# Retention and a rational feed-forward block on one core: a list scheduler in the kernel sets the order of all engines, and decoding's words move from PSUM to SBUF

## The chip, the core and the metric

The kernel runs on one core of a Trainium2 chip, whose engines run side by side, each through its own queue in order: TensorE (PE: matmuls, and PEld: weight loads), VectorE (DVE), ScalarE (ACT), GpSimd (POOL), and SyncE (SP), which here issues every DMA. The metric is device microseconds of one execution. Lower is better.

## What is computed

A retention (linear attention with a decay for each head) over batch 4, 8 heads, 768 positions and 64 dimensions, and then a feed-forward block with a rational activation on the 3072 tokens of 512 values:

```
for t in range(S):
    state = gamma * state + k[:, :, t] outer v[:, :, t]
    y[:, :, t] = scale * q[:, :, t] @ state            # x: (3072, 512)
h = x @ w_in                                           # 512 -> 2048
P = a[0] + a[1]*h + a[2]*h**2 + a[3]*h**3
Q = 1 + |b[0]|*|h| + |b[1]|*h**2
out = (P / (Q + 1e-6)) @ w_out                         # 2048 -> 512
```

The weights arrive as 8-byte words, and the kernel decodes them to float32 on the chip.

## The kernel before

**Work.** The tokens are 24 chunks of 128 (6 for each of 4 batches), 4 chunks make a block of 512 tokens, 6 blocks in all. The hidden 2048 are 16 tiles f of 128. A *slot* is one pair (block n, tile f), 96 of them. Blocks 0 and 1 go through tiles 0 to 7 and then 8 to 15 (half sums of the output go to DRAM and come back); blocks 2 to 5 go through all 16.

**A chunk of retention.** TensorE computes scores `pa` (`scores`), VectorE masks them into `aT` (`mask`), GpSimd scales v (`scale_v`) and the state (`scale_state`). TensorE adds into `px` what the state recalls (`recall`), the values (`values_early`, `values_late`) and, for the next state, k outer v (`outer`). VectorE scales `px` (L329), ScalarE rounds it to `xh` (L330), VectorE forms the remainder `xl` (L334). Chunks follow each other through the state.

**A slot.** `gemm_in` (L392) multiplies xh, xl with the two parts of w_in's tile into a bank `ph`: 12 matmuls. ScalarE takes |h| (L403), q's inner term s (L409, or on GpSimd L405 where a tile is decoded and no chunk is due) and p (L411). GpSimd forms q = q*s (L410), VectorE the polynomial (L415, L416), ScalarE the reciprocal from a root (L420, L421), VectorE refines and multiplies (L424 to L426). The last one frees the bank `ph`, of which there are two. ScalarE rounds the result to `gh` (L431), GpSimd forms the remainder `gl` (L432), and `gemm_out` (L447) multiplies both with w_out's tile into four banks `po`: 12 matmuls.

**Decoding a weight tile** (32 tiles of 512 KB): ScalarE makes `t` from the word's low byte (L130) and `u` from its high half (L138), VectorE joins them (L146, L149), ScalarE rounds to `w` (L159), GpSimd forms the remainder (L166). `u` lives in a PSUM bank, which `u_bank` picks: early in free banks, later in the two that `pa` and `px` use too.

**Order.** It is written out by hand: `opening` does chunks 0 to 3 with two filler matmuls in each chunk and 10 ahead (they compute nothing that is used), and `run` then goes through the slots, one tile decoded in each, with the second product three slots behind (`LAG = 3`). Loads go out in program order on SP.

Of the kernel before, what the change touches and what calls it, by code (L numbers as in the profile page):

```python
# [7 lines left out]
F32 = mybir.dt.float32  # L8
F32R = mybir.dt.float32r
# [8 lines left out]
TB = 512  # L18


@with_exitstack
def tile_retention_rational_ffn(
# [24 lines left out]
    NB = NSTEP // SPB  # L47

# [16 lines left out]

    def early_bank(name, tag, dtype=F32):
        pool = ps_o if tag.startswith("po") else ps
        return pool.tile([P, TB], dtype, name=name, tag=tag)

    def u_bank():  # L70

        if not opened:
            return early_bank("u", "ph0", U32)
        if len(opened) < 2:
            count["u"] += 1
            return early_bank("u", f"po{count['u'] % 2}", U32)
# [24 lines left out]
    lead, HF = 4, NF // 2  # L101
    tiles = []
    for h in range(0, NF, HF):
        tiles += [(0, h + f) for f in range(lead)]
        for f in range(h, h + HF):
            tiles += [(1, f)] + [(0, f + lead)] * (f + lead < h + HF)
    raws = []

    def fetch(count=1):
        for m, f in tiles[len(raws) : len(raws) + count]:  # L110
            raw = wp.tile([P, DM, 2], U32, name="raw", tag=f"w{m}_{f}")
            nc.sync.dma_start(
                out=raw.rearrange("p m w -> p (m w)"), in_=(w_in, w_out)[m][f]
            )
            raws.append(raw)

    us, ts = {}, {}

    def decode_read(i):
        decode_low(i)  # L120
        decode_high(i)

    def decode_low(i):
        if i >= len(tiles):
            return


        ts[i] = ff.tile([P, DM], U32, name="t", bufs=3)
        byte = raws[i].rearrange("p m w -> p (m w)").bitcast(U8)[:, 3::8]
        nc.scalar.activation(ts[i], byte, AF.Identity, bias=lcon[:, 0:1], scale=1.0 / 32)  # L130

    def decode_high(i):
        if i >= len(tiles):
            return


        us[i] = u_bank()
        nc.scalar.activation(  # L138
            us[i].bitcast(F32), raws[i][:, :, 1].bitcast(F32), AF.Abs, scale=2.0 ** -112
        )  # L140

    def decode_join(i):
        if i >= len(tiles):
            return
        u = us.pop(i)
        nc.vector.scalar_tensor_tensor(  # L146
            u, u, 3, ts[i], ALU.logical_shift_left, ALU.bitwise_or
        )
        nc.vector.scalar_tensor_tensor(  # L149
            ts[i], raws[i][:, :, 1], 0x80000000, u, ALU.bitwise_and, ALU.bitwise_or  # L150
        )

    def decode_split(i):
        if i >= len(tiles):
            return
        m, f = tiles[i]

        w = (w1, w2)[m][f] = wp.tile([P, 2, DM], F32R, name="w", tag=f"w{m}_{f}")
        nc.scalar.copy(w[:, 0], ts[i].bitcast(F32))  # L159

    def decode_rest(i):
        if i >= len(tiles):
            return
        m, f = tiles[i]
        w = (w1, w2)[m][f]
        nc.gpsimd.tensor_sub(w[:, 1], ts.pop(i).bitcast(F32), w[:, 0].bitcast(F32))  # L166


    steps = {}
    x_tiles = {}  # L170

    def x_block(n):
        if n not in x_tiles:
            x_tiles[n] = (
                xp.tile([P, NP, TB], F32R, name="xh"),
                xp.tile([P, NP, TB], F32R, name="xl"),
            )
        return x_tiles[n]

    borrowed = {2: ("gh", "gh", "q", "gl", "s"), 3: ("gh", "gl", "q", "gl", "s")}

    def landing(i, which, name, shape):
        if i in borrowed:
            tag = borrowed[i][which]
            full = ff.tile([P, TB], F32, name=name, tag=tag, bufs=BUFS.get(tag, 2))
            return full.rearrange("p (a b) -> p a b", b=shape[2])[:, : shape[1]]
        return at.tile(shape, F32, name=name)

    def load_part(i, n, src, which, shape):
# [8 lines left out]
    def load_again(i):  # L200
        if i % C > 0:
            load_part(i, "q2T", q2T, 4, [P, 2, P])

    def load_rest(i):
        load_part(i, "qT", qT, 1, [P, NP, P])
        load_again(i)
        load_part(i, "v", v, 3, [P, H, D])
        if i % C < C - 1:
            load_part(i, "k", kk, 2, [P, H, D])

    def scale_v(i):
        st = steps[i]
        nc.gpsimd.tensor_mul(  # L218
            st["v"], st["v"], vdec_sb.unsqueeze(2).broadcast_to([P, H, D])
        )  # L220

    def scale_state(i):
        if i % C > 0:
            nc.gpsimd.tensor_mul(
                state, state, sdec_sb.unsqueeze(2).broadcast_to([P, NP, D])
            )
# [10 lines left out]
    def scores(i):  # L237
        st = steps[i]
        pa = [bank("pa")[:, : 6 * D].rearrange("p (j t) -> p j t", t=3 * D) for _ in range(2)]
        for j in range(2):  # L240
            for a in range(2):
                whole, part = [], []
                for s in range(2):
                    r = s ^ a
                    kt, qt = (st[n][half(s), 2 * a + j] for n in ("kT", "qT"))
                    to = pa[s][half(r), j, : 3 * D if a != s else 2 * D]
                    if a != s:
                        to = to.rearrange("p (x t) -> p x t", t=D)[:, ::2]
                        qt = qt.rearrange("p (x t) -> p x t", t=D)
                    whole.append((to, kt[:, :D], qt))  # L250
                    qt = st["qT"][half(s), 2 * a + j]
                    part.append((pa[s][half(1 - r), j, later(a, s)], kt[:, D:], qt[:, D:]))
                for to, kt, qt in part + whole if a else whole + part:
                    nc.tensor.matmul(to, kt, qt, start=True, stop=True, skip_group_check=True)  # L254
        st["pa"] = pa

    def mask(i):
        st = steps[i]
        for s in range(2):
            st["aT", s] = at.tile([P, 2, 3 * D], F32, name="aT")  # L260
            nc.vector.tensor_mul(
                st["aT", s], st["pa"][s],
                causal_sb.rearrange("p x t -> p (x t)").unsqueeze(1).broadcast_to([P, 2, 3 * D]),
            )

    def outer(i, early=False):
        st = steps[i]
        px = st["px"]
        if i % C < C - 1:
            pk = st["pk"] = px[1][:, TB // 2 :].rearrange("p (h d) -> p h d", d=D)  # L270
            for aj in range(NP):
                for r in range(2):
                    h = 4 * (aj // 2) + 2 * r + aj % 2
                    nc.tensor.matmul(  # L274
                        pk[half(r), aj], st["k"][:, h], st["v"][:, h],
                        start=(i % C == 0 or early), stop=True, skip_group_check=True,
                    )

    def recall(i):
        st = steps[i]  # L280
        if i % C > 0:

            for a in range(2):
                for j in range(2):
                    for r in range(2):
                        qt = st["q2T"][half(r), j] if a else st["qT"][half(r), j]
                        nc.tensor.matmul(  # L287
                            st["px"][r][half(j), a * P : (a + 1) * P], state[half(r), 2 * a + j], qt,
                            start=(a == 0), stop=False, skip_group_check=True,
                        )  # L290
# [392 lines left out]
```

## Time and profile before

| | us |
|---|---|
| median of 3 runs | 639.15 (638.56 to 639.27) |
| profiled execution, its time | 639.73 |
| its span in the profile | 638.0 |
| TensorE busy | 611.7 (96%) |
| VectorE busy | 452.9 (71%) |
| ScalarE busy | 441.4 (69%) |
| GpSimd busy | 334.2 (52%) |

A row of the table by stretches has, for each engine, its busy time in that stretch and how many instructions; then the clock that TensorE was granted (1.00 is full), the share of time in which the DMA engines were busy, and GB/s. A row of a timeline has start, duration, engine, line, operation and operands, with the idle time ahead of it and what ended that in brackets. A row of the groups has line, engine, operation, operands, count, then busy us and mean ns of one, then the idle time ahead and what ended it.

### The profile page before, as it was taken

The numbers are of one execution on the slowest core, as the hardware profiler recorded it, in microseconds if no ns is written. First come the engines' busy times: TensorE is split into PE (matmuls) and PEld (weight loads), VectorE is DVE, ScalarE is ACT, GpSimd is POOL, SyncE is SP. The second block draws the span as 40 slices with busy tenths as digits, with TensorE's granted clock in tenths as the row PEclk, the third lists the DMA queues.
The fourth block names the chain that finished last, engine by engine and source line by source line (L and its number), as shares of the span: only waits on it lengthen the run. The fifth ranks groups of instructions, "written<-read, shape, count | busy, mean of one in ns | idle before, by whom it ended". The sixth has DMA issues, their size and how long they took to land.

```text
span 638.0 us, 11577 instructions
## 1 busy us (share of the span) xinstructions
PE 611.7 (96%) x4506; PEld 494.4 (77%) x4510; DVE 452.9 (71%) x731; ACT 441.4 (69%) x721; POOL 334.2 (52%) x288
## 2 busy tenths in 40 slices
PE   6766999999999999999999999999999999999997
PEld 4655778888877878788888888888878888888885
DVE  3778688888888666785666777667766766666664
ACT  2488789888886665567666675766766666777773
POOL 1566568887875543454453454535354443444442
PEclk9887999999999999999999999999999999999999
DMA  8995563101015232320120311111311000100001
GB/s 306 393 370 174 192 241 141 44 1 66 1 45 180 87 96 85 124 76 17 59 59 17 116 44 61 48 27 54 112 40 43 2 0 1 42 25 2 0 2 66
DMA packets 27270, 55.11 MB, mean 86 GB/s; under 512 B 3408, under 2 KB 6096, under 8 KB 27216
## 3 DMA queue, kind: packets, MB, share of 16 engines
q1 hardware_dynamic: 27216, 54.38, 25.1%
q8 instruction: 35, 0.57, 0.4%
q14 instruction: 19, 0.16, 0.1%
HBM read 45.98 MB, written 8.39 MB: 85 GB/s over the span
## 4 chain that ended last, share of the span: by engine, by line
PE 67%; ACT 13%; DVE 11%; issue 5%; DMA 2%; POOL 1%; SPq 1%; POOLq 0%; DVEq 0%; ACTq 0%
PE po L447 30%; PE ph L392 30%; ACT t L130 3%; ACT s L420 2%; ACT ph L421 2%; DVE q L424 2%; PE pa L254 2%; DVE p L426 2%; DVE ph L425 2%; PE px L308 2%; DMA v<-in_v 2%; PE px L287 2%; PE px L274 1%; ACT u L138 1%; ACT s L409 1%
## 5 line engine op out<-in xcount | busy, mean ns | idle before, releaser
L410 POOL TENSOR_TENSOR q<-q,s 128x512 f32<-128x512 f32 x96 | 124.4, 1296 | 224.1 <-ACT s L409 215.4
L392 PE MATMUL ph<-xh,w 128*128 128x512 f32 (+2 forms) x776 | 210.4, 393 | 10.1 <-DVE p L426 5.7
L447 PE MATMUL po<-w,gh 128*128 128x512 f32 x768 | 201.4, 394 | 0.0
L392 PEld LDWEIGHTS ph<-xh,w 128*128 128x128 f32 x776 | 143.8, 188 | 42.5 <-DVE t L149 3.0
L447 PEld LDWEIGHTS po<-w,gh 128*128 128x128 f32 x768 | 143.4, 189 | 30.7 <-POOL w L166 0.2
L403 ACT ACTIVATE q<-ph 128x512 f32<-128x512 f32 x96 | 57.2, 596 | 111.3 <-PE ph L392 111.2
L415 DVE TENSOR_TENSOR p<-ph,p 128x512 f32<-128x512 f32 x96 | 66.2, 689 | 94.1 <-ACT p L411 94.1
L432 POOL TENSOR_TENSOR gl<-p,gh 128x512 fp32r<-128x512 f32 x96 | 124.4, 1295 | 9.7 <-ACT gh L431 3.8
L447 PE MATMUL po<-w,gl 128*128 128x512 f32 x384 | 111.1, 391 | 0.2 <-POOL gl L432 0.2
L424 DVE SCALAR_TENSOR_TENSOR q<-q,small,ph 128x512 f32<-128x512 f32 x96 | 71.4, 744 | 47.3 <-ACT ph L421 47.2
L392 PE MATMUL ph<-xl,w 128*128 128x512 f32 (+2 forms) x388 | 104.1, 390 | 0.0
L420 ACT ACTIVATE s<-q,small 128x512 f32<-128x512 f32 x96 | 69.4, 723 | 22.7 <-POOL q L410 22.7
L392 PEld LDWEIGHTS ph<-xl,w 128*128 128x128 f32 x388 | 73.2, 189 | 15.4
L447 PEld LDWEIGHTS po<-w,gl 128*128 128x128 f32 x384 | 72.5, 189 | 15.8 <-POOL gl L432 0.6
L416 DVE SCALAR_TENSOR_TENSOR p<-p,small,ph 128x512 f32<-128x512 f32 x96 | 71.8, 748 | 3.4
L411 ACT ACTIVATE p<-ph,small 128x512 f32<-128x512 f32 x96 | 73.2, 762 | 0.0
L425 DVE SCALAR_TENSOR_TENSOR ph<-p,small,ph 128x512 f32<-128x512 f32 x96 | 72.0, 750 | 0.0
L431 ACT CAST gh<-p 128x512 fp32r<-128x512 f32 x96 | 58.6, 610 | 16.7 <-DVE p L426 16.7
L426 DVE SCALAR_TENSOR_TENSOR p<-q,ph 128x512 f32<-128x512 f32 x96 | 65.9, 687 | 3.3
L409 ACT ACTIVATE s<-q,small 128x512 f32<-128x512 f32 x80 | 65.3, 816 | 2.7
L421 ACT ACTIVATE ph<-s 128x512 f32<-128x512 f32 x96 | 57.8, 602 | 9.9 <-DVE p L416 0.8
L218 POOL TENSOR_TENSOR v<-v,small 128x512 f32<-128x512 f32 x24 | 25.0, 1044 | 41.8 <-DMA v<-in_v 40.1
(41 smaller groups left out, 439.8 us busy)
## 6 DMA issues: line engine op xcount, KB each, us to landing
raw<-in_w_in SPq DMA_DIRECT2D x16, 512.0 KB, 5.7
raw<-in_w_out SPq DMA_DIRECT2D x16, 512.0 KB, 7.3
kT<-in_kT SPq DMA_DIRECT2D x24, 256.0 KB, 2.8
qT<-in_qT SPq DMA_DIRECT2D x24, 256.0 KB, 3.2
v<-in_v SPq DMA_DIRECT2D x24, 256.0 KB, 3.6
out<-o SPq DMA_DIRECT2D x24, 256.0 KB, 2.1
k<-in_k SPq DMA_DIRECT2D x20, 256.0 KB, 3.9
q2T<-in_q2T SPq DMA_DIRECT2D x20, 128.0 KB, 3.2
```

What stands on the lines that cost most here:

```text
L392: nc.tensor.matmul(ph[:, t0:t1], w1[f][:, part, kt * P : (kt + 1) * P], x[:, kt, t0:t1], start=(i == 0), stop=(i == 3 * NP - 1),)
L409: nc.scalar.activation(s, q, AF.Identity, bias=babs[:, 0:1], scale=babs[:, 1:2])
L410: nc.gpsimd.tensor_mul(q, q, s)
L411: nc.scalar.activation(p, ph, AF.Identity, bias=par_sb[:, 2:3], scale=par_sb[:, 3:4])
L416: nc.vector.scalar_tensor_tensor(p, p, par_sb[:, 1:2], ph, ALU.add, ALU.mult)
L420: nc.scalar.activation(s, q, AF.Abs_reciprocal_sqrt, bias=qcon[:, 0:1])
L421: nc.scalar.activation(ph, s, AF.Square)
L424: nc.vector.scalar_tensor_tensor(q, q, qcon[:, 0:1], ph, ALU.add, ALU.mult)
L425: nc.vector.scalar_tensor_tensor(ph, p, par_sb[:, 0:1], ph, ALU.add, ALU.mult)
L426: nc.vector.scalar_tensor_tensor(p, q, 2.0, ph, ALU.subtract, ALU.mult, reverse0=True)
L432: nc.gpsimd.tensor_sub(gl, p, gh.bitcast(F32))
L447: nc.tensor.matmul(o_tiles[n][tt], g_[:, tt * P : (tt + 1) * P], w2[f][:, part], start=(first and m == 0), stop=(last and m == 2),)
```

## The change

All steps become objects: each has the engines that may run it, a cost, the steps that it follows, a rank, the buffers that it takes and those that it uses. `Plan.order` then repeats: for each engine it finds the step that could begin first by its own clock of costs, takes among those within `LOOK` of it the one of lowest rank, and issues the earliest over all engines. The order so found is the program's order. The arithmetic and the number of its instructions stay, but for filler matmuls and where the step s runs. What is different beside the order:

- `u` of the decoding is an SBUF tile of the pool that also holds outputs (`o`, 4 buffers), and no PSUM bank.
- The banks: ph has b0 and b1, pa and px have pairs of the others (b2 and b3 once two first products are under way), po has b4 to b7.
- The step s may go to GpSimd or ScalarE in slots below `SHARED = 30`, whichever can begin first (19 go to GpSimd, 16 before).
- The second product's rank is its slot plus 3.6 (`OUT`); it runs when it is ready and no step of lower rank is.
- In the opening the k outer v of chunks 1 to 3 is a step of its own, and scores may run up to two chunks ahead.
- Fillers go wherever the plan sees a gap on TensorE of 0.6 us or more before the first product.

```diff
+class Plan:
+    def ready(self, x):
+        t = 0
+        for a, early in x.after:
+            if a.start is None:
+                return None
+            t = max(t, a.start if early is None else a.end - early + WAKE)
...
+    def order(self, before=None):
+        waiting = list(self.steps)
+        while waiting:
...
+                for e in x.engines:
+                    start = max(t, self.free.get(e, 0))
+                    if e == "SP" and len(self.landings) >= LANES:
+                        start = max(start, self.landings[-LANES])
+                    by_engine.setdefault(e, []).append((start, x.rank, len(by_engine), x))
+            for e, found in by_engine.items():
+                first = min(f[0] for f in found)
+                start, rank, _, x = min(
+                    (f for f in found if f[0] <= first + LOOK.get(e, 0)), key=lambda f: (f[1], f[0])
+                )
+                if best is None or start < best[0]:
+                    best = start, e, x
...
-        us[i] = u_bank()
-        nc.scalar.activation(
-            us[i].bitcast(F32), raws[i][:, :, 1].bitcast(F32), AF.Abs, scale=2.0 ** -112
-        )
+            cell["u"] = ff.tile([P, DM], U32, name="u", tag="o", bufs=BUFS["o"])
+            nc.scalar.activation(
+                cell["u"].bitcast(F32), cell["raw"][:, :, 1].bitcast(F32), AF.Abs, scale=2.0 ** -112
+            )
...
+        L = step(("ACT",), (651, 761), low, [got], rank, [t])
+        U = step(("ACT",), (548, 623), high, [got, L], rank - 0.001, [u])
+        J = step(("DVE",), (1300, 1385), join, [L, U], rank, uses=[t, u])
+        S = step(("ACT",), (509, 607), split, [J], rank - 0.002, uses=[t])
+        R = step(("POOL",), (1249, 1295), rest, [S], rank, uses=[t])
...
+        A1 = turn("A1", step(("ACT",), (490, 600), a1, [G], k, [q], [ph]))
+        engines = ("ACT", "POOL") if k < SHARED else ("ACT",)
+        A2 = turn("A2", step(engines, {"ACT": (720, 820), "POOL": (771, 771)}, a2, [A1, ready["babs"]], k, [s], [q]))
+        A3 = turn("A3", step(("ACT",), (660, 760), a3, [G, A1, ready["par"]], k, [p], [ph]))
+        P1 = step(("POOL",), (1250, 1297), p1, [A2], k, uses=[q, s])
+        D1 = step(("DVE",), (1440, 1440), d1, [A3], k, uses=[p, ph])
+        A4 = step(("ACT",), (1265, 1327), a4, [P1, D1], k, uses=[q, s, ph])
+        D2 = step(("DVE",), (2030, 2100), d2, [A4, D1], k, uses=[p, q, ph])
+        A6 = turn("A6", step(("ACT",), (526, 610), a6, [D2], k, [gh], [p]))
+        P2 = turn("P2", step(("POOL",), (1253, 1297), p2, [A6], k, [gl], [p, gh]))
...
+        slack = 450 if first or final else 1800
+        O = step(
+            ("PE",), 2720, run_out,
+            [A6, (P2, slack), s1, (r1, slack), G, *gemms_out[-1:]], k + OUT,
+            [po] if first else [], [gh, gl] + ([] if first else [po]),
+        )
...
+LOOK = {"ACT": 100, "DVE": 100, "POOL": 100}
+EARLY = 2
+SHARED = 30
+OUT = 3.6
+AHEAD = 1.0
```

On SP's queue, the loads from chunk 1 to the first load of chunk 3 (kT, qT, q2T, v, k are a chunk's; raw is a weight tile). Before:

```order
L195 DMA kT<-in_kT 128x512
L195 DMA qT<-in_qT 128x512
L195 DMA q2T<-in_q2T 128x256
L195 DMA v<-in_v 128x512
L195 DMA k<-in_k 128x512
L112 DMA raw<-in_w_in 128x1024
L195 DMA kT<-in_kT 128x512
L195 DMA qT<-in_qT 128x512
L195 DMA q2T<-in_q2T 128x256
L195 DMA v<-in_v 128x512
L195 DMA k<-in_k 128x512
L112 DMA raw<-in_w_in 128x1024
```

Now:

```order
L221 DMA q2T<-in_q2T 128x256
L221 DMA raw<-in_w_in 128x1024
L221 DMA kT<-in_kT 128x512
L221 DMA qT<-in_qT 128x512
L221 DMA v<-in_v 128x512
L221 DMA k<-in_k 128x512
L221 DMA q2T<-in_q2T 128x256
L221 DMA kT<-in_kT 128x512
L221 DMA qT<-in_qT 128x512
L221 DMA v<-in_v 128x512
L221 DMA k<-in_k 128x512
L221 DMA q2T<-in_q2T 128x256
```

Before, tile 0 of w_in went out with chunk 0 and another tile followed each chunk. Now tile 0 goes out behind chunk 1, chunks 2 and 3 follow without a tile between them, and tile 1 comes behind the first two loads of chunk 4.

On ScalarE, from slot 0's first step (q from ph) to its rounding gh. Before:

```order
L403 ACTIVATE q<-ph 128x512
L409 ACTIVATE s<-q,small 128x512
L411 ACTIVATE p<-ph,small 128x512
L159 CAST w<-t 128x512 x2
L420 ACTIVATE s<-q,small 128x512
L421 ACTIVATE ph<-s 128x512
L130 ACTIVATE t<-raw,small 128x512
L138 ACTIVATE u<-raw 128x512
L403 ACTIVATE q<-ph 128x512
L409 ACTIVATE s<-q,small 128x512
L411 ACTIVATE p<-ph,small 128x512
L431 CAST gh<-p 128x512
```

Now:

```order
L491 CAST w<-t 128x512
L582 ACTIVATE p<-ph,small 128x512
L491 CAST w<-t 128x512
L472 ACTIVATE t<-raw,small 128x512
L567 ACTIVATE q<-ph 128x512
L596 ACTIVATE s<-q,small 128x512
L599 ACTIVATE ph<-s 128x512
L582 ACTIVATE p<-ph,small 128x512
L476 ACTIVATE u<-raw 128x512
L472 ACTIVATE t<-raw,small 128x512
L476 ACTIVATE u<-raw 128x512
L611 CAST gh<-p 128x512
```

The step s of slots 0 and 1 is gone from ScalarE (GpSimd has it), and slot 1's q (the second L403, now the L567 shown; slot 0's stands just ahead) has moved from behind slot 0's ratio steps to ahead of them.

On TensorE, from slot 2's first product on. Before, up to slot 3's first product:

```order
L392 MATMUL ph<-xh,w 128x512 x4
L392 MATMUL ph<-xl,w 128x512 x4
L392 MATMUL ph<-xh,w 128x512 x4
L254 MATMUL pa<-qT,kT 64x128
L254 MATMUL pa<-qT,kT 64x2x64
L254 MATMUL pa<-qT,kT 64x64 x4
L254 MATMUL pa<-qT,kT 64x2x64
L254 MATMUL pa<-qT,kT 64x128 x2
L254 MATMUL pa<-qT,kT 64x2x64
L254 MATMUL pa<-qT,kT 64x64 x4
L254 MATMUL pa<-qT,kT 64x2x64
L254 MATMUL pa<-qT,kT 64x128
```

Now:

```order
L512 MATMUL ph<-xh,w 128x512 x4
L512 MATMUL ph<-xl,w 128x512 x4
L512 MATMUL ph<-xh,w 128x512 x4
L527 MATMUL po<-w,gh 128x512 x2
L527 MATMUL po<-w,gl 128x512
L527 MATMUL po<-w,gh 128x512 x2
L527 MATMUL po<-w,gl 128x512
L527 MATMUL po<-w,gh 128x512 x2
L527 MATMUL po<-w,gl 128x512
L527 MATMUL po<-w,gh 128x512 x2
L527 MATMUL po<-w,gl 128x512
```

Slot 0's second product now stands right behind slot 2's first product; before, a chunk's scores, slot 3's first product and the rest of that chunk stood between them.

More of the change, by code (lines that the diff above doesn't have):

```diff
@@ L18, with __init__ @@
 TB = 512
+LANES = 8
+WAKE = 60
+ARRAY = 163
+ISSUE, LATENCY, LANDED, RATE = 470, 1850, 900, 380
+class Buffer:
+    def __init__(self, pool, options=None):
+        self.pool, self.options, self.users, self.banks = pool, options, [], None
+class Step:
+    def __init__(self, engines, cost, run, after, rank, takes):
+        self.engines, self.cost, self.run, self.rank, self.takes = engines, cost, run, rank, takes
+        self.after = [(a, 0) if isinstance(a, Step) else a for a in after if a]
+        self.start = self.end = None
@@ L153, in decode_split @@
[L153 to L178, printed above, removed]
@@ L222, in scale_state, with psum @@
[L222 to L226, printed above, removed]
+    plan = Plan({**BUFS, "x": 2}, [f"b{i}" for i in range(8)])
+    step = plan.step
+    nc.vector.memset(zeros, 0.0)
+    nc.vector.memset(qcon, 1.0 + 1e-6)
+    nc.vector.memset(lcon, -15.5 / 32)
+    nc.scalar.activation(babs[:, 0:1], qcon, AF.Abs_reciprocal_sqrt)
+    def psum(buffer, i, name, dtype=F32):
+        return ps.tile([P, TB], dtype, name=name, tag=buffer.banks[i])
@@ new lines, in tile_retention_rational_ffn, with free_banks, pairs, load @@
+    opened = {"in": 0}
+    def free_banks():
+        names = ["b2", "b3"]
+        if opened["in"] < EARLY:
+            names += ["b4", "b5", "b6", "b7"]
+        if not opened["in"]:
+            names += ["b0"]
+        return names
+    def pairs():
+        names = free_banks()
+        return [names[i : i + 2] for i in range(0, len(names) - 1, 2)]
+    def load(dst, src, nbytes, rank, takes=(), uses=(), after=()):
+        cell = {}
+        def run(_):
+            cell["tile"] = dst()
+            nc.sync.dma_start(out=cell["tile"], in_=src())
+        x = step(("SP",), (ISSUE, max(nbytes / RATE, 190)), run, after, rank, takes, uses)
+        return x, cell
@@ L235, in later, with scores @@
         return slice(D, 2 * D) if a == s else slice(2 * D, 3 * D)
-    def scores(i):
-        st = steps[i]
-        pa = [bank("pa")[:, : 6 * D].rearrange("p (j t) -> p j t", t=3 * D) for _ in range(2)]
+    def scores(st):
         for j in range(2):
@@ L257, in mask, with outer @@
[L257 to L271, printed above, removed]
+    def outer(st, c, first):
+        for aj in range(NP):
+            for r in range(2):
+                h = 4 * (aj // 2) + 2 * r + aj % 2
+                nc.tensor.matmul(
+                    st["pk"][half(r), aj], st["k"][:, h], st["v"][:, h],
+                    start=(c == 0 or first), stop=True, skip_group_check=True,
+                )
@@ L437, in gemm_out, with gemm_in @@
+    o_tiles = {}
+    def gemm_in(cell, n, f, t0, t1):
+        xh, xl = x_tiles[n]
+        i = 0
+        for part, x in ((0, xh), (0, xl), (1, xh)):
+            for kt in range(NP):
+                nc.tensor.matmul(
+                    cell["ph"][:, t0:t1], w[0, f][:, part, kt * P : (kt + 1) * P], x[:, kt, t0:t1],
+                    start=(i == 0), stop=(i == 3 * NP - 1),
+                )
+                i += 1
+    def gemm_out(cell, n, f, first, last, po):
         if first:
-            o_tiles[n] = [ps_o.tile([P, DM], F32, name="po", tag=f"po{i}") for i in range(SPB)]
@@ L479, in tile_retention_rational_ffn @@
-    groups = {
-        (n, f): (f == 0 or (n < 2 and f == HF), f == NF - 1 or (n < 2 and f == HF - 1))
-        for n, f in order
-    }
-    parts = {}
+    starts = {}
     for n in range(1, NB):
```

749 lines of the change are left out of this document (401 added, 348 removed).

## The prediction

> **What bounds the kernel now.** I read the page's head first, then the table of busy time by stretches, then the order of time on single engines around the opening, then the groups of instructions.
>
> ```profile
> span 638.0 us, 11577 instructions
> PE 611.7 (96%) x4506; PEld 494.4 (77%) x4510; DVE 452.9 (71%) x731; ACT 441.4 (69%) x721; POOL 334.2 (52%) x288
> ...
> core 0: us, PE busy (x) PEld busy (x) DVE busy (x) ACT busy (x) POOL busy (x), PEclk, DMA share, GB/s
> 0.00:26.00 26.00, 18.97 (x382) 12.62 (x386) 12.57 (x31) 8.63 (x17) 8.60 (x14) 0.93 0.94 339
> 26.00:44.00 18.00, 11.62 (x141) 9.54 (x135) 13.02 (x24) 12.93 (x23) 10.22 (x9) 0.91 1.00 386
> 44.00:64.00 20.00, 14.27 (x117) 11.18 (x118) 17.55 (x32) 17.32 (x31) 13.97 (x12) 0.83 0.59 207
> 64.00:110.00 46.00, 45.31 (x347) 36.26 (x346) 37.22 (x62) 37.54 (x64) 29.81 (x27) 1.00 0.54 189
> 110.00:160.00 50.00, 49.97 (x221) 41.05 (x220) 44.88 (x67) 44.63 (x77) 41.33 (x37) 1.00 0.12 43
> 160.00:630.00 470.00, 467.57 (x3298) 381.14 (x3297) 326.33 (x519) 319.11 (x511) 229.00 (x191) 1.00 0.16 50
> 630.00:638.00 8.00, 3.94 (x17) 2.60 (x15) 1.38 (x2) 1.24 (x3) 1.29 (x1) 0.90 0.35 131
> ```
>
> TensorE is idle 638.0 - 611.7 = 26.3 us, and the stretches say where: 7.0 before 26, 6.4 from 26 to 44, 5.7 from 44 to 64, then 0.7 over 46 us, nothing over 50, 2.4 over 470 us, and 4.1 in the tail. From 64 us on TensorE itself is the bound. A change of order, which leaves its matmuls alone, can therefore gain only in the first 64 us (19.1 us idle, with a granted clock of 0.83 to 0.93), and it can lose anywhere that another engine falls behind. The other engines stand at 88% (VectorE 17.55 of 20) and 87% (ScalarE) just before 64, and at 83 to 90% from 110 to 160, so there is little slack for a loss.
>
> The opening in order of time:
>
> ```profile
> 17.20 1.04 POOL L218 TENSOR_TENSOR v<-v,small 128x512 f32<-128x512 f32 x1 [3.97 <-DMA v<-in_v]
> ...
> 20.63 0.63 PE L350 MATMUL idle<-zeros 128*128 128x512 bf16 x1 [0.34 <-issue]
> ...
> 25.29 0.76 DVE L334 TENSOR_TENSOR xl<-px,xh 128x256 fp32r<-128x256 f32 x2 [0.16 <-ACT xh L330]
> ...
> 26.11 0.96 PE L392 MATMUL ph<-xh,w 128*128 128x384 f32 x4
> ...
> 29.61 0.82 PE L392 MATMUL ph<-xh,w 128*128 128x128 f32 x4 [1.14 <-ACT xh L330]
> ...
> 30.79 0.61 PE L392 MATMUL ph<-xh,w 128*128 128x128 f32 x4
> ...
> 34.67 0.58 ACT L403 ACTIVATE q<-ph 128x512 f32<-128x512 f32 x1
> ...
> 43.14 0.69 DVE L426 SCALAR_TENSOR_TENSOR p<-q,ph 128x512 f32<-128x512 f32 x1
> ...
> 43.98 1.17 PE L392 MATMUL ph<-xh,w 128*128 128x512 f32 x4 [2.36 <-DVE p L426]
> ...
> 59.44 1.22 PE L447 MATMUL po<-w,gh 128*128 128x512 f32 x2
> ...
> 109.42 0.39 PE L447 MATMUL po<-w,gl 128*128 128x512 f32 x1
> ...
> 109.65 1.07 PE L392 MATMUL ph<-xh,w 128*128 128x512 f32 x4
> ...
> 115.09 1.08 PE L392 MATMUL ph<-xh,w 128*128 128x512 f32 x4
> ```
>
> Slot 0's first product ends at 31.4, but ScalarE takes it up only at 34.67, behind two tiles' decoding; slot 0's last VectorE step ends at 43.83, and slot 2's product, which needs that bank, waits for it till 43.98. The first product with w_out starts at 59.44, though its operands are older. The last product of the first half ends at 109.65; by then slots 0 to 10 have their first product and slots 0 to 7 their second. A slot costs TensorE 115.09 - 109.65 = 5.44.
>
> **Start of slot 0.** The queue takes only one w_in tile ahead of chunk 2's v instead of two: 0.52 MB at 339 GB/s, 1.5 us, so v is scaled from 15.7 and not 17.2. The outer products follow at 16.7, the scores of chunk 3 now come next (0.9), the recall, and chunk 2's values end near 20.2 instead of 22.5; the filler ahead of them (0.63 and its gap) has moved to the front. State 0.42, two scalings 0.75, half of the next mask 0.55 and xl 0.76 give 22.7 for the first piece, against 26.11. Chunk 3's recall and values then stand behind this piece and not ahead: 22.7 + 2.05 for the piece, 2.05 for them, 2.5 for the same VectorE steps, 1.8 for the second piece (29.61 to 31.4) is 31.0. What is won in front is thus given back: 31.0 against 31.4.
>
> **Slot 0 to its last VectorE step.** ScalarE now takes slot 0's product up at once, VectorE has both operands of slot 0 by the time slot 1's product ends (31.0 + 2.7), and slot 1's absolute value stands ahead of slot 0's two ratio steps: 33.7 + 0.9 + 1.3, then three VectorE steps 2.2 and hops give 38.3 instead of 43.83, 5.5 us. Tiles 1 to 3 of w_in come later than before, by some 2 MB of chunks moved ahead of them; at 386 GB/s w_in tile 1 lands near 21 and tile 2 near 24, before they are needed, so I cost this at nothing; if that cover goes, each us goes to the end.
>
> **From there VectorE sets the pace.** Durations:
>
> ```profile
> L410 POOL TENSOR_TENSOR q<-q,s 128x512 f32<-128x512 f32 x96 | 124.4, 1296 | 224.1 <-ACT s L409 215.4 <-PE px L274 5.7 <-PE pa L254 1.6
> ...
> L425 DVE SCALAR_TENSOR_TENSOR ph<-p,small,ph 128x512 f32<-128x512 f32 x96 | 72.0, 750 | 0.0
> L416 DVE SCALAR_TENSOR_TENSOR p<-p,small,ph 128x512 f32<-128x512 f32 x96 | 71.8, 748 | 3.4
> L424 DVE SCALAR_TENSOR_TENSOR q<-q,small,ph 128x512 f32<-128x512 f32 x96 | 71.4, 744 | 47.3 <-ACT ph L421 47.2
> ...
> L415 DVE TENSOR_TENSOR p<-ph,p 128x512 f32<-128x512 f32 x96 | 66.2, 689 | 94.1 <-ACT p L411 94.1
> L426 DVE SCALAR_TENSOR_TENSOR p<-q,ph 128x512 f32<-128x512 f32 x96 | 65.9, 687 | 3.3
> ...
> L431 ACT CAST gh<-p 128x512 fp32r<-128x512 f32 x96 | 58.6, 610 | 16.7 <-DVE p L426 16.7
> ...
> L130 ACT ACTIVATE t<-raw,small 128x512 uint32<-128x512 uint8 x33 | 25.1, 761 | 6.2 <-DMA raw<-in_w_in 6.2
> ...
> L261 DVE TENSOR_TENSOR aT<-pa,causal_sb 128x384 f32<-128x384 f32 x48 | 24.6, 552 | 7.1 <-PE pa L254 7.0
> L146 DVE SCALAR_TENSOR_TENSOR u<-u,t 128x512 uint32<-128x512 uint32 x32 | 22.2, 693 | 7.1 <-ACT u L138 7.1
> L149 DVE SCALAR_TENSOR_TENSOR t<-raw,u 128x512 uint32<-128x512 uint32 x32 | 22.0, 688 | 1.3
> ...
> L334 DVE TENSOR_TENSOR xl<-px,xh 128x256 fp32r<-128x256 f32 x48 | 18.2, 420 | 7.1 <-ACT xh L330 6.9
> L329 DVE TENSOR_TENSOR px<-px,xdec_sb 128x256 f32<-128x256 f32 x48 | 18.1, 423 | 0.0
> ```
>
> Between the last steps of slots 0 and 7 VectorE's new order holds 7 slots x (0.689 + 0.748 + 0.744 + 0.750 + 0.687) = 25.3, 13 decoded tiles x (0.693 + 0.688) = 18.0 (7 tiles before: decoding is pulled forward), 16 scalings and remainders of x 6.7, 6 masks 3.3, three state steps of about 0.42: 54.6 us. TensorE's own work there is 15 products of 2.72 and three chunks of about 3, 50 us, and hides beneath it. The instructions overlap a little, which I leave as the allowance for stalls. Slot 7's last step is then at 38.3 + 54.6 = 92.9; its cast 0.6, its product 2.9 and hops end at 96.8. Two first products fewer are done by then than at 109.65 before, so the like moment before is 109.65 - 2 x 2.72 = 104.2. Gain 7.4.
>
> **Slots 8 to 15.** ScalarE has 77 instructions there; the 77 from 110 to 160 us kept it busy 44.6. TensorE's eight slots take 43.5. So 1.1 us are lost. The denominator step moved to GpSimd for more of the first 30 slots is counted in this: GpSimd is at 83% from 110 to 160 and stays hidden; if it did not, the wait would fall on the ratio steps and on VectorE behind them.
>
> **Steady part and tail.** The order of products from slot 31 on is the same, as are the three products left after the last first product, and the queue of loads still runs two chunks ahead. I cost it at zero; the 2.4 us idle there bound a gain, and the same again a loss.
>
> **The words in SBUF.** ScalarE writes u to SBUF instead of PSUM, and two VectorE instructions of each of 32 tiles now read two SBUF operands. No VectorE group of this trace with 512 columns does so: each has a PSUM operand. Below, all neighbours lie between 0.687 and 0.750, so nothing is to be saved; above, an instruction could wait for GpSimd: half a GpSimd instruction, 0.65, times its share of time, 41.33 of 50, is 0.54 for each, on 64 of them. I take the value of the nearest rows, L146 and L149, which is no change.
>
> The Trainium skill's page "SBUF — State Buffer", section "Who interferes with whom", speaks against this: a VectorE instruction with two SBUF inputs takes its second input through a read interface that it shares with GpSimd, and contends with a GpSimd instruction that reads SBUF. No row of before has such a pair, so the trace can't say; by that rule the second rival would be the forecast.
>
> **Sum.** -7.4 + 1.1 = -6.3. The profiled execution took 639.73, which gives 633.4; the median of the runs stands 0.6 lower, so 633 us. About 0.2%, 1.3 us, is what a measurement here can tell from no change.
>
> **Rivals.**
> - The opening gains more. VectorE's steps follow each other 5% faster than their durations (2.7 us), slots 8 to 15 lose nothing (1.1) and the idle 2.4 of the steady part goes: 627 and a little below. For it: 19.1 us stand idle in the opening. Against: three engines would be above 90% at once.
> - Contention on the words. 26 of the instructions stand before slot 7's last step, where VectorE is the pace, and 24 more in slots 8 to 15, where it has no slack either. At 0.54 on VectorE alone that is +27, 660; with half of it taken by GpSimd, +14, 647. From 0.13 each (6.3 / 50) the gain is gone, beyond it the kernel is slower. For it: GpSimd reads SBUF 83% of the time there. Against: the rows L146 and L149 show nothing of GpSimd's being busy, though with one SBUF operand only.
> - The order is right only on paper: ScalarE's and GpSimd's queues are in order, and a tile that lands 5 us late holds slot 0's steps behind its decoding. 38.3 becomes 43 and the gain 1 to 2: 638. For it: the queues move 386 GB/s at a share of 1.00 then. Against: before, ScalarE's t steps (L130) waited for a tile once, 6.2 us at the start.
> - A wait in the steady part, where loads, stores and scaled v share queues in a new order: two stalls of 3 us on top of the third, 643.
>
> **Chances.** Forecast, 628 to 637: 0.41. More gained: 0.06. Contention: 0.34, mostly 641 to 660. Gain eaten: 0.13, mostly within 0.2%. A new wait: 0.06. Faster 0.48, same 0.10, slower 0.42. The range for 8 in 10 is 626 to 656; the forecast's own is 628 to 637.
>
> **What would show it.** Slot 0's last VectorE step near 38 and slot 2's product right behind it; the first product with w_out near 41 instead of 59; idle TensorE before 64 us down to some 13; VectorE above 90% from 40 to 95; the two word steps still at 0.69 each. It is wrong if these two lengthen (or GpSimd's 1.296 does), if TensorE shows idle time from 64 to 160, or if tiles land behind ScalarE's demand.

## The result: 658.5 us, 3.1% slower

The changed kernel takes 658.49 us (median; 658.09 to 659.85) against 638.86 for the kernel before on the same chip: ratio 1.0311, 95% interval 1.0293 to 1.0329. The forecast was 633. The page's busy times of the changed kernel, then its table by stretches, which up to 160 us is cut where the forecast's table is cut:

```profile
span 658.1 us, 11588 instructions
...
PE 619.3 (94%) x4504; PEld 497.7 (76%) x4507; DVE 482.4 (73%) x731; ACT 438.3 (67%) x716; POOL 351.0 (53%) x291
```

```profile
core 0: us, PE busy (x) PEld busy (x) DVE busy (x) ACT busy (x) POOL busy (x), PEclk, DMA share, GB/s
0.00:26.00 26.00, 18.55 (x356) 13.24 (x363) 12.49 (x30) 8.09 (x16) 8.16 (x13) 1.00 0.92 318
26.00:44.00 18.00, 13.89 (x177) 11.25 (x167) 14.04 (x24) 13.89 (x26) 12.88 (x12) 0.81 1.03 400
44.00:64.00 20.00, 18.87 (x177) 14.12 (x175) 19.63 (x31) 15.41 (x28) 15.16 (x13) 1.00 0.99 378
64.00:110.00 46.00, 35.09 (x255) 26.91 (x256) 45.03 (x59) 31.96 (x55) 38.11 (x30) 0.89 0.33 120
110.00:160.00 50.00, 43.08 (x170) 34.28 (x170) 45.48 (x55) 40.30 (x68) 37.89 (x30) 0.90 0.06 22
160.00:650.00 490.00, 485.79 (x3371) 395.21 (x3370) 344.33 (x535) 327.32 (x527) 237.48 (x196) 1.00 0.16 50
```

VectorE has the same 731 instructions and is busy 29.5 us longer; GpSimd has three more and is busy 16.8 us longer. The opening did get better: TensorE has 51.3 us of work in the first 64, against 44.9 before. From 64 to 110 VectorE is full (45.03 of 46), TensorE idles 10.9 us there (0.7 before) and another 6.9 up to 160 (0.03 before), and its granted clock drops to 0.89 and 0.90. The groups of instructions name the place where VectorE's time went (the two words of decoding, and for comparison an instruction of a slot; then GpSimd's remainder of a weight tile, L166 of before, where it took 1293 ns):

```profile
L605 DVE SCALAR_TENSOR_TENSOR p<-q,ph 128x512 f32<-128x512 f32 x96 | 65.9, 687 | 3.3
...
L494 POOL TENSOR_TENSOR w<-t,w 128x512 fp32r<-128x512 f32 x32 | 44.7, 1401 | 11.3 <-ACT w L491 11.2
L485 DVE SCALAR_TENSOR_TENSOR t<-raw,u 128x512 uint32<-128x512 uint32 x32 | 40.5, 1265 | 1.7
L482 DVE SCALAR_TENSOR_TENSOR u<-u,t 128x512 uint32<-128x512 uint32 x32 | 33.2, 1038 | 1.5 <-ACT u L476 1.5
```

L482 and L485 are L146 and L149 of before, with u in SBUF: 33.2 + 40.5 = 73.7 us instead of 22.2 + 22.0 = 44.2, which is +29.5, all that VectorE gained. L605, with the PSUM operand `ph`, stays at 687 ns. The timeline shows one tile's words beside GpSimd (start, duration):

```profile
81.35 0.69 DVE L605 SCALAR_TENSOR_TENSOR p<-q,ph 128x512 f32<-128x512 f32 x1
81.45 1.31 POOL L494 TENSOR_TENSOR w<-t,w 128x512 fp32r<-128x512 f32 x1
...
81.95 1.35 DVE L482 SCALAR_TENSOR_TENSOR u<-u,t 128x512 uint32<-128x512 uint32 x1
...
82.70 1.75 POOL L587 TENSOR_TENSOR q<-q,s 128x512 f32<-128x512 f32 x1
...
83.34 1.66 DVE L485 SCALAR_TENSOR_TENSOR t<-raw,u 128x512 uint32<-128x512 uint32 x1
...
84.41 1.74 POOL L615 TENSOR_TENSOR gl<-p,gh 128x512 fp32r<-128x512 f32 x1
84.92 0.68 DVE L590 TENSOR_TENSOR p<-ph,p 128x512 f32<-128x512 f32 x1
```

L605 and L590, with a PSUM operand, run beside the same GpSimd instructions undisturbed. The two words take 1.35 and 1.66 us instead of 0.69, and the two GpSimd instructions that begin while a word runs (L587, L615) take 1.75 and 1.74 instead of 1.30; L494, which began ahead of the word, takes 1.31. So it is in the whole trace: the 10 of the 64 words that meet no GpSimd instruction take 678 to 693 ns, and each of the words over 693 ns began while a GpSimd instruction was running. What TensorE makes of it, first in the table of its waits over the whole run (before, then the change), then in its timeline where slot 7's last step frees the bank:

```profile
PE ph L392 <- DVE p L426: 5.7, 5, 2.4
```

```profile
PE ph L512 <- DVE p L605: 23.7, 9, 6.0
```

```profile
104.17 2.07 PE L512 MATMUL ph<-xh,w 128*128 128x512 f32 x4 [6.00 <-DVE p L605]
106.04 1.91 PE L512 MATMUL ph<-xl,w 128*128 128x512 f32 x4
107.75 1.77 PE L512 MATMUL ph<-xh,w 128*128 128x512 f32 x4
109.36 0.63 PE L527 MATMUL po<-w,gh 128*128 128x512 f32 x2
```

A row has the us in total, the number of waits and the longest. Nine waits for a slot's last VectorE step make 23.7 us (5.7 before), and after the 6.0 us wait the product of 12 matmuls lasts 5.2 us, at a granted clock of 0.51, where one lasts 2.72 at full clock. So the loss has two parts: against before, TensorE is idle 38.8 instead of 26.3 us (+12.5) and busy 619.3 instead of 611.7 (+7.6), together the 20.1 us of the spans.

### The profile page after: what moved, and what is told of

It is laid out like the page before. It is cut to its first block, busy times and chain, and to the rows that moved or that the text cites. A ratio compares the mean times of both kernels' runs of the same rounds, so it can differ in the third digit from the quotient of the medians.

```text
span 658.1 us, 11588 instructions
## 1 busy us (share of the span) xinstructions
PE 619.3 (94%) x4504; PEld 497.7 (76%) x4507; DVE 482.4 (73%) x731; ACT 438.3 (67%) x716; POOL 351.0 (53%) x291
## 4 chain that ended last, share of the span: by engine, by line
PE 74%; DVE 6%; ACT 3%; issue 2%; POOLq 0%; DVEq 0%; ACTq 0%
PE ph L512 35%; PE po L527 33%; PE pa L257 2%; PE px L290 1%; PE px L273 1%; DVE u L482 1%; PE px L263 1%; DVE q L603 1%; DVE ph L604 1%; DVE p L605 1%; DVE t L485 1%; PE px L282 1%; DVE p L590 0%; DVE p L591 0%; ACT ph L599 0%
## 5 line engine op out<-in xcount | busy, mean ns | idle before, releaser
L512 PE MATMUL ph<-xh,w 128*128 128x512 f32 (+2 forms) x776 | 216.5, 402 | 26.3 <-DVE p L605 23.7
L587 POOL TENSOR_TENSOR q<-q,s 128x512 f32<-128x512 f32 x96 | 126.6, 1319 | 196.5 <-ACT s L576 187.7
L512 PEld LDWEIGHTS ph<-xh,w 128*128 128x128 f32 x776 | 148.9, 195 | 61.7 <-DVE p L605 20.2
L527 PEld LDWEIGHTS po<-w,gh 128*128 128x128 f32 x768 | 141.9, 188 | 31.6 <-ACT gh L611 0.6
L615 POOL TENSOR_TENSOR gl<-p,gh 128x512 fp32r<-128x512 f32 x96 | 128.9, 1343 | 46.9 <-ACT gh L611 33.9
L567 ACT ACTIVATE q<-ph 128x512 f32<-128x512 f32 x96 | 57.3, 596 | 117.2 <-PE ph L512 117.2
L590 DVE TENSOR_TENSOR p<-ph,p 128x512 f32<-128x512 f32 x96 | 66.0, 688 | 60.4 <-ACT p L582 60.1
L512 PE MATMUL ph<-xl,w 128*128 128x512 f32 (+2 forms) x388 | 108.0, 402 | 0.0
L512 PEld LDWEIGHTS ph<-xl,w 128*128 128x128 f32 x388 | 75.9, 196 | 16.3
L596 ACT ACTIVATE s<-q,small 128x512 f32<-128x512 f32 x96 | 69.5, 724 | 25.7 <-POOL q L587 25.7
L605 DVE SCALAR_TENSOR_TENSOR p<-q,ph 128x512 f32<-128x512 f32 x96 | 65.9, 687 | 3.3
L611 ACT CAST gh<-p 128x512 fp32r<-128x512 f32 x96 | 58.6, 611 | 12.7 <-DVE p L605 12.2
L576 ACT ACTIVATE s<-q,small 128x512 f32<-128x512 f32 x77 | 62.8, 816 | 2.1
L494 POOL TENSOR_TENSOR w<-t,w 128x512 fp32r<-128x512 f32 x32 | 44.7, 1401 | 11.3 <-ACT w L491 11.2
```

The source lines that it names most:

```text
L512: nc.tensor.matmul(cell["ph"][:, t0:t1], w[0, f][:, part, kt * P : (kt + 1) * P], x[:, kt, t0:t1], start=(i == 0), stop=(i == 3 * NP - 1),)
L527: nc.tensor.matmul(o_tiles[n][tt], g_[:, tt * P : (tt + 1) * P], w[1, f][:, part], start=(first and m == 0), stop=(last and m == 2),)
L576: nc.scalar.activation(cell["s"], cell["q"], AF.Identity, bias=babs[:, 0:1], scale=babs[:, 1:2])
L587: nc.gpsimd.tensor_mul(cell["q"], cell["q"], cell["s"])
L590: nc.vector.tensor_mul(cell["p"], cell["ph"], cell["p"])
L596: nc.scalar.activation(cell["s"], cell["q"], AF.Abs_reciprocal_sqrt, bias=qcon[:, 0:1])
```

## The experiments

**Theory:** the list's order is worth about what was forecast; the words that read two SBUF operands collide with GpSimd, and that costs some 26 us. **Rivals:** the order itself loses (too many tiles decoded early, too much s on GpSimd), or the banks do. All ratios are to the kernel before on the same chip. Where the words are replaced (5 to 8), the weights are other numbers, so that these runs tell of time alone.

**1. The collision by itself** (only these instructions; the retention and the feed-forward block are left out). Rows of 12 word instructions with u in PSUM (`pu`) or in SBUF, beside a row of one GpSimd operation, and alone:

```diff
+for _ in range(44): nc.gpsimd.tensor_sub(o, g, h)
+for _ in range(12): stt(pu, pu, 3, t, SL, OR)
+for _ in range(12): stt(u, u, 3, t, SL, OR)
+for _ in range(12): stt(t, raw[:, :, 1], 0x80000000, u, AND, OR)
...
```

> A measurement alone, which leaves the whole computation out: 12 VectorE instructions each of the two word steps (u shifted and joined with t; sign bits of raw joined with u) and of the old form (one operand in PSUM), beside a stream of GpSimd tensor_tensor, beside nothing, and the first one beside GpSimd tensor_scalar (one input) and memset (no input). Contention theory: 0.69 us for the PSUM form everywhere and for all forms beside nothing and beside memset; 1.2 to 2.0 us for the SBUF forms beside tensor_tensor, less beside tensor_scalar, and GpSimd's 1.30 us lengthens at the same time. Order theory: 0.69 everywhere, so that the long instructions of the changed kernel have another cause.

Groups of this kernel. L76 is GpSimd's row that runs beside L78, L80, L82; L92 runs beside L94, L97 beside L99; L85, L87, L89 and L103 are alone:

```profile
L76 POOL TENSOR_TENSOR o<-g,h 128x512 f32<-128x512 f32 x44 | 63.4, 1441 | 3.5
L82 DVE SCALAR_TENSOR_TENSOR t<-raw,u 128x512 uint32<-128x512 uint32 x12 | 19.6, 1634 | 0.4
L80 DVE SCALAR_TENSOR_TENSOR u<-u,t 128x512 uint32<-128x512 uint32 x12 | 19.5, 1625 | 0.4
...
L103 POOL TENSOR_TENSOR o<-g,h 128x512 f32<-128x512 f32 x12 | 15.1, 1262 | 0.9
...
L94 DVE SCALAR_TENSOR_TENSOR u<-u,t 128x512 uint32<-128x512 uint32 x12 | 11.2, 932 | 0.4
L78 DVE SCALAR_TENSOR_TENSOR pu<-pu,t 128x512 uint32<-128x512 uint32 x12 | 8.4, 699 | 0.4
...
L99 DVE SCALAR_TENSOR_TENSOR u<-u,t 128x512 uint32<-128x512 uint32 x12 | 8.3, 692 | 0.4
L87 DVE SCALAR_TENSOR_TENSOR u<-u,t 128x512 uint32<-128x512 uint32 x12 | 8.3, 691 | 0.4
```

The word instructions take 691 and 693 ns alone and 1625 and 1634 beside GpSimd's tensor_tensor; the first of them takes 692 beside GpSimd's memset, which reads nothing, and 932 beside its tensor_scalar. With the PSUM operand it takes 699 beside that tensor_tensor. The collision is a matter of the operand's place. In such rows, one instruction behind the other, it costs 0.93 to 0.94 us for each; in the kernel it depends on what a word meets (675 to 1752 ns for L482). The rule of the Trainium skill ("SBUF — State Buffer", "Who interferes with whom") says just this of two SBUF inputs against a GpSimd instruction that reads SBUF, and not against one that only writes; the runs agree.

**2. The SBUF tile alone, in the hand-written order.**

```diff
-        us[i] = u_bank()
+        us[i] = ff.tile([P, DM], U32, name="u", tag="o", bufs=BUFS["o"])
```

> The kernel before in its hand-written order; only u lies in the SBUF pool of the outputs (4 buffers), as in the changed kernel, instead of a PSUM bank. Contention theory: the stand-alone measurement gave 1.63 us for a word instruction beside a GpSimd tensor_tensor and 0.69 beside nothing, so both lengthen to 0.9 to 1.4, VectorE is 20 to 30 us busier, and the time is 648 to 662. Order theory: words at 0.69, time 638 to 641.

651.56 us, ratio 1.0184 (1.0158 to 1.0211). The groups:

```profile
L166 POOL TENSOR_TENSOR w<-t,w 128x512 fp32r<-128x512 f32 x32 | 47.8, 1498 | 0.0
L149 DVE SCALAR_TENSOR_TENSOR t<-raw,u 128x512 uint32<-128x512 uint32 x32 | 39.6, 1238 | 1.7 <-DVE u L146 0.5
...
L146 DVE SCALAR_TENSOR_TENSOR u<-u,t 128x512 uint32<-128x512 uint32 x32 | 25.3, 791 | 7.5 <-ACT u L138 7.5
```

The words take 64.9 us instead of 44.2, and the kernel loses 12.5 us without any list. This part of the change costs time in either order.

**3. The list alone, with u in a PSUM bank** that the plan picks from the free ones.

```diff
-        t, u = Buffer("t"), Buffer("o")
+        t, u = Buffer("t"), Buffer("psum", lambda: [[b] for b in free_banks()])
...
-            cell["u"] = ff.tile([P, DM], U32, name="u", tag="o", bufs=BUFS["o"])
+            cell["u"] = psum(u, 0, "u", U32)
```

> The changed kernel with its list scheduler; only u goes back to PSUM, to a bank that the plan picks from those that pa and px may use. The plan then finds another order. Contention theory: the word instructions are back at 0.69, VectorE some 29 us less busy, and the time is 630 to 642, since slot 0 to 3 were already earlier with the list order. Order theory: 652 to 660, as the changed kernel.

658.58 us, ratio 1.0305 (1.0249 to 1.0361): a miss for the theory as it was put. The words are back at 693 and 688 ns, but the plan now finds another order. TensorE's waits from 26 to 200 us:

```profile
PE ph L512 <- DVE p L605: 8.8, 3, 5.6
PE pa L257 <- issue: 6.9, 1, 6.9
PE px L273 <- DVE t L485: 6.1, 1, 6.1
PE po L527 <- ACT gh L611: 4.5, 2, 2.4
```

("issue" is time in which TensorE waited for nothing that the profile shows.) Once two first products have begun, u and the chunks' pairs share only b2 and b3, and the chunks of the next block come late behind decoding: 28.08 us of TensorE's work from 64 to 110 instead of 45.31. This doesn't clear the order; it only shows that the list can't simply be given the bank back. Hence the runs 5 to 8, which keep the changed kernel's order word for word, and 9 and 10, which repair the bank.

**4. s on ScalarE alone** (`SHARED = 0`; the plan gives another order).

> The changed kernel with the denominator step s on ScalarE in all slots (19 were on GpSimd, 17 us). Contention theory: GpSimd is a little less busy, so the words wait a little less; ScalarE is some 16 us busier: 652 to 660. Share theory (GpSimd's extra 17 us are what costs): below 648.

653.11 us, ratio 1.0198 (1.0161 to 1.0236). Some 7 of the 20 us go, with GpSimd's share in s and with the other order, and 13 stay: the words still take 1124 and 1026 ns, 68.8 us together. So the shared step isn't the whole cause; what it adds, this run can't separate from the order. Run 8 can: it shares s as the change does and loses nothing.

**5. One SBUF input each, same order.** Both words become tensor_scalar instructions on `raw` and constants.

```diff
-            nc.vector.scalar_tensor_tensor(u_, u_, 3, t_, ...)
+            nc.vector.tensor_scalar(u_, cell["raw"][:, :, 1], 3, 1, ...)
...
-            nc.vector.scalar_tensor_tensor(t_, cell["raw"][:, :, 1], 0x80000000, u_, ...)
+            nc.vector.tensor_scalar(t_, cell["raw"][:, :, 1], 0x80000000, 0x3E000000, ...)
```

> The changed kernel in exactly its order; the two word instructions read one SBUF operand (raw) and constants, so t and u are not joined and the weights are other numbers. Contention theory: the words are at 0.7 or below, VectorE is some 30 us less busy, TensorE's idle time from 64 to 200 us goes, and the time falls to 628 to 636. Order theory: 652 to 658, since the order is the same.

639.32 us, ratio 1.001 (0.9993 to 1.0028). 19 of the 20 us are gone, but not the collision: these two took 702 and 1002 ns in the mean, from 407 and up to 1589. The 15 that meet no GpSimd instruction took 410 to 428 ns, and each of those over 430 began while one was running, so one SBUF input isn't safe in every operation. With 54.6 us for the two, the run doesn't show the order without collisions.

**6. Writes in place of the words, same order** (the weights are a constant): nothing is read.

```diff
-            nc.vector.scalar_tensor_tensor(u_, u_, 3, t_, ...)
-            nc.vector.scalar_tensor_tensor(t_, cell["raw"][:, :, 1], 0x80000000, u_, ...)
+            nc.vector.memset(u_.bitcast(F32), 0.125)
+            nc.vector.memset(t_.bitcast(F32), 0.125)
+            nc.vector.memset(t_.bitcast(F32), 0.125)
```

> The list's order and SBUF tiles as in the changed kernel; only the two joining words of each weight tile are left out, and three writes of a constant by VectorE stand in their place (no operand is read; the weights are the constant 0.125). Contention theory (the words that read two SBUF operands lose to GpSimd, and the order alone would have gained): the 29.5 us of VectorE's time go, the words cost 1.4 to 1.5 us a tile, TensorE's waits for VectorE's last step of a slot shrink to single us between 64 and 160, and the time is 628 to 636 us. Rival (the order itself loses, since 13 tiles are decoded before slot 7): 64 to 110 us still has under 39 us of TensorE, the time is 640 to 650.

637.56 us, ratio 0.9963 (0.9942 to 0.9983). Every write took 485 ns, so nothing collides. The time lies between the two expectations (628 to 636, and 640 to 650 for the rival). Three writes take 1.68 us of VectorE in the mean from the first one's start to the last one's end, longer than the words undisturbed (1.42 before); run 8 does without that.

**7. Only the first word as a write;** the second stays and reads two SBUF operands. 

> As the changed kernel, with only the first of the two words of each tile left out (one write of a constant in its place); the second word still reads two SBUF operands, and the weights are other values. Contention theory by dose: the second word stays at a mean of 1.1 to 1.3 us, VectorE's time is 12 to 19 us over the kernel before, and the time is 640 to 650 us, between the changed kernel and the one with writes alone. Rival (the joining words' length does not matter, the order does): within 4 us of the one with writes alone.

637.35 us, ratio 0.9961 (0.9941 to 0.9980): no half dose, but within 4 us of run 6, as the rival had it. The remaining word took 947 ns in the mean, 30.3 us, and the write 15.5; their sum, 45.8 us, is less than run 6's 46.5, since the write is shorter than the word it replaces. The expected numbers were wrong because the saving had been left out; the run tells nothing apart.

**8. Writes that last as long as the words, same order** (in place of the same two words).

```diff
+            nc.vector.memset(cell["raw"].rearrange("p m w -> p (m w)")[:, :1000].bitcast(F32), 0.125)
+            nc.vector.memset(t_.bitcast(F32), 0.125)
```

> As the run with three writes in place of the two words, but the writes now last as long as the words do where nothing disturbs them: one of 1000 elements into the spent raw tile (0.89 us, estimated from 0.272 us for 256 and 0.485 us for 512) and one of 512 into t (0.485 us), together 1.38 us a tile against some 1.7 us from the first one's start to the last one's end there. The weights are the constant 0.125. If the order's own gain is the forecast's 6.3 us and the three writes hid part of it: slots 7 to 15 take 46 to 47 us instead of 50.2, and the time is 631 to 635 us. Rival (the order in slots 8 to 15 loses 4 us by itself, with its two tiles more than before): those slots stay at 49 to 51 us and the time is 636 to 639.

632.90 us, ratio 0.9905 (0.9882 to 0.9927), where the forecast for the change was 633. The page's head, the two writes, and the stretches:

```profile
span 631.0 us, 11579 instructions
...
PE 608.2 (96%) x4507; PEld 492.1 (78%) x4507; DVE 453.6 (72%) x731; ACT 437.2 (69%) x716; POOL 336.5 (53%) x291
```

```profile
L482 DVE MEMSET raw<- 128x1000 f32 x32 | 28.5, 892 | 6.1 <-issue 4.0 <-ACT u L476 1.4 <-ACT xh L445 0.2
...
L483 DVE MEMSET t<- 128x512 f32 x32 | 15.5, 485 | 1.8
```

```profile
0.00:64.00 64.00, 52.07 (x711) 40.26 (x711) 45.63 (x89) 41.16 (x73) 37.76 (x40) 0.95 0.99 367
64.00:110.00 46.00, 40.49 (x291) 31.69 (x290) 41.95 (x70) 40.70 (x71) 38.78 (x36) 0.96 0.37 134
110.00:160.00 50.00, 48.83 (x212) 39.36 (x212) 44.17 (x66) 46.42 (x79) 41.18 (x35) 1.00 0.12 42
160.00:625.00 465.00, 464.69 (x3290) 379.39 (x3289) 320.49 (x506) 307.76 (x494) 218.82 (x183) 1.00 0.15 48
```

The time is the expected one, 631 to 635; the expected 46 to 47 us for slots 7 to 15 isn't met, for they take 48.9, near the rival's 49 to 51. The order and the instructions' number are those of the change, and VectorE's work (453.6 us, 452.9 before) is that of the words without the collision: from start to end a tile's two writes take 1.43 us in the mean, the words 1.42 before. GpSimd's L490, the former L494, is back at 1296 ns. The two spans differ by 27.1 us: 16.0 are TensorE's idle time (38.8 against 22.8), 11.1 its longer busy time (619.3 against 608.2). The collision costs 4.1% (1.0311 less 0.9905), 26 us, and the order gains 6.1 (4.7 to 7.5). With run 6's longer writes as the measure it would be 22 and 2.4. Run 8 has the change's banks, its SBUF pool for u, its sharing of s and its early decoding, so none of these costs the 26 us. That constant weights speed TensorE up isn't tested by itself; run 10 has the true ones, and TensorE is busy for 606.7 us there, 608.2 here.

In one table, the runs with the changed kernel's own order; the time rises with what VectorE spends on the words, though not in proportion:

| words or what stands for them | us of VectorE, 32 tiles | ratio |
|---|---|---|
| two writes as long as the words (8) | 44.0 | 0.9905 |
| one write, one word (7) | 45.8 | 0.9961 |
| three writes (6) | 46.5 | 0.9963 |
| two tensor_scalar (5) | 54.6 | 1.0010 |
| the change | 73.7 | 1.0311 |

**9. A list that keeps u in PSUM.** To run 3's edit comes a gate: a tile's decoding waits until the first product `LEAD = 7` tiles ahead of it has begun, so that u doesn't take the chunks' banks early.

```diff
+            for i, tile_ in enumerate(tiles):
+                if i - LEAD == k:
+                    lows[tile_].after.append((gemms_in[k], None))
```

> The list order with u in PSUM, and each tile's decoding held back until seven slots before its place in the hand-written series, so that u takes the two shared banks less often while chunks need them as a pair. Bank theory (the list order with u in PSUM was slow because chunks 5 to 7 waited for a pair of banks): 640 to 652, TensorE idle from 64 to 110 below 12 us instead of 18. If the order has another fault: 655 or more.

637.51 us, ratio 0.9983 (0.9958 to 1.0009): better than expected, and level with before.

**10. More banks for longer, and decoding ranked later.** Run 9 with `EARLY = 4` (b4 to b7 stay free for u and chunks until four first products have begun), and then also with `AHEAD = 0.5`.

> The list with u in a PSUM bank and decoding held to 7 slots ahead, and now b4 to b7 free to u and to chunks until four first products have begun, not two. If the 6.1 us that TensorE waits for VectorE and the 4 us that it waits for words and masks between 26 and 110 us come from pairs of banks that u holds: chunks 4 to 6 come earlier and the time is 632 to 636 us. Rival (those waits come from VectorE's amount of work there, which the banks do not change): 636 to 639, as without the edit.

633.91 us, ratio 0.9904 (0.9882 to 0.9927).

> As the run before it, and every decoding step ranked half a slot later, so that a slot's own steps go ahead of decoding more often. If decoding ahead of need is what delays the first slots' last steps: 1 to 2 us faster than the run before it, 631 to 635 us. Rival (it only moves which slot waits): the same within 1 us.

632.06 us, ratio 0.9880 (0.9844 to 0.9916), the fastest whole kernel of the study: 7.7 us under before (5.4 to 10.0), and 4.3% under the change (1.0311 less 0.9880). The intervals of the two runs overlap, so what the later rank adds isn't settled. Its page's head and its stretches from 64 us on:

```profile
span 629.6 us, 11591 instructions
...
PE 606.7 (96%) x4504; PEld 491.6 (78%) x4507; DVE 454.7 (72%) x731; ACT 440.0 (70%) x719; POOL 334.2 (53%) x288
```

```profile
64.00:110.00 46.00, 44.43 (x317) 35.50 (x316) 39.38 (x64) 38.24 (x66) 35.17 (x31) 1.00 0.37 133
110.00:160.00 50.00, 49.87 (x217) 40.06 (x216) 43.20 (x65) 47.22 (x79) 38.18 (x33) 1.00 0.12 43
```

Its words are at 695 and 688 ns and TensorE is nearly full from 64 us on, at full clock. Run 3's loss was a matter of when u takes the banks (run 9) and of their number and the ranks (run 10), not of the list.

## Why the prediction was wrong

The step that failed is "The words in SBUF", the sentence "I take the value of the nearest rows, L146 and L149, which is no change". Both rows have u in PSUM. A PSUM operand is just what keeps an instruction clear of GpSimd (699 against 1625 ns in run 1), so they could not speak for a kernel without it. The same paragraph had the right mechanism and nearly the right size: it bounded the loss at 0.54 us for each of 64 instructions; measured were 0.35 for the first word and 0.58 for the second, 0.46 in the mean, far beyond the 0.13 from which the gain was gone. The contention rival, given 0.34, is what happened: its upper end, 660, is 1.5 us from the time. That it comes so near is partly luck: its 27 us are VectorE's time alone, while 11.1 of the 27.1 us between the change and run 8 are TensorE's longer busy time, which was no term of it. The rule that the prediction cites from the Trainium skill ("SBUF — State Buffer", "Who interferes with whom") and sets aside was the right one to follow: "by that rule the second rival would be the forecast".

The other steps, by the changed kernel and by run 8, where nothing collides. Slot 7's last step, the forecast's main term, first in the change and then in run 8:

```profile
103.43 0.69 DVE L605 SCALAR_TENSOR_TENSOR p<-q,ph 128x512 f32<-128x512 f32 x1
```

```profile
91.46 0.69 DVE L601 SCALAR_TENSOR_TENSOR p<-q,ph 128x512 f32<-128x512 f32 x1
```

| step | forecast | change | run 8 |
|---|---|---|---|
| first piece of slot 0's product begins | 22.7 | 22.5 | 22.7 |
| TensorE idle before 64 us | 13 | 12.7 | 11.9 |
| slot 0's last VectorE step ends | 38.3 | 41.8 | 39.1 |
| first product with w_out begins | 41 | 44.8 | 43.4 |
| slot 7's last step ends | 92.9 | 104.1 | 92.2 |
| from there to slot 15's, against 45.9 before | +1.1 | +12.4 | +3.0 |
| sum against before | -6.3 | +19.6 | -6.1 |

- **Start of slot 0 and TensorE's idle time in the opening:** right, in the change too.
- **Slot 0's last step:** in run 8 0.8 us late. In the change it is 3.5 late, and the step named next holds it: slot 1's absolute value stands ahead of slot 0's two ratio steps on ScalarE, and slot 1's product ends at 37.7 instead of 33.9 in run 8, since TensorE's granted clock is 0.50 from 30.72 to 37.55 (1.00 in run 8). The forecast's sum has 2.7 us for that product. TensorE had waited 1.77 us just before (0.92 in run 8); that the colliding words behind this wait, as the one of 1.55 us at 25.74, are its cause fits, but isn't shown by itself.
- **VectorE sets the pace from slot 0 to slot 7:** right. In the change it is busy 61.09 of the 62.3 us between these two steps, decoding the 13 tiles that were counted; the late start (3.5) and these tiles' words (29.5 us instead of the forecast's 18.0) more than cover the 11.2 us by which slot 7 is late. In run 8 it is busy 49.6 of 53.1 us, where 54.6 were forecast.
- **Slots 8 to 15:** the term was mis-sized, and its pace-setter is doubtful. It was put at ScalarE and +1.1 us; without the collision it is +3.0. TensorE still waits there for VectorE's last steps, with ScalarE busy 45.0 and VectorE 42.8 of 48.8 us. In the sum the 1.5 us that slots 0 to 7 were shorter made up for part of it, and the rest isn't accounted for, so that 6.1 against 6.3 agrees better than its terms do: that is luck in part.
- **Steady part and tail at zero:** right; in run 8 TensorE is busy 464.69 of the 465 us from 160 on.
- **s on GpSimd:** hidden as costed as far as the runs show, since run 8 has it; but in the change each GpSimd instruction more is one more to collide with, which run 4 fits and doesn't prove, as its order differs.

## What to carry to other kernels

Moving an operand from PSUM to SBUF is no free change of place: look whether the instruction then has two SBUF inputs while GpSimd reads SBUF, and price it by a measurement of that pair, not by rows that lack the condition. Where the nearest row differs in exactly the property that a documented rule names, the row is no evidence against the rule. And to judge a new order, keep it word for word and replace the suspect instructions by ones of equal length that can't collide: a kernel that plans its own order changes it with every edit of its resources, as run 3 did.

## What the runs showed of the hardware

- The collision slows both sides: beside each other in rows the VectorE word goes from 691 to 1625 ns, while GpSimd's tensor_tensor goes from 1262 to a median of 1588 ns. In the kernel the one that begins second is the long one (L494 1.31 us ahead of a word, L587 and L615 1.75 and 1.74 behind one).
- VectorE's tensor_scalar, with a single SBUF input, was stretched as well (410 to 428 ns clear of GpSimd, up to 1589 beside it, run 5); a write alone was not (485 ns each time, run 6).
- The price of a wait on TensorE can be more than the wait. After 6.0 us idle, 12 matmuls took 5.2 us instead of 2.72, at a granted clock of 0.51; after 2.33 us, at 41.98, they took 2.80 at 1.00, but after 2.74, at 75.67, 4.23 at 0.66, and the half clock from 30.72 on followed a wait of only 1.77. While the granted clock was 0.50, TensorE was busy for 26.5 us in the change and for 9.6 in run 8; half of the difference, 8.5 us by this estimate, is most of the 11.1 us by which its busy time differs.
